# Three conversions moved behind attention's last copy, and two kinds of differences moved from VectorE to GpSimd

## The chip, the cores and the metric

One core of a Trainium2 chip runs one program that holds three stages: attention, a first mixture layer (MoE 1) and a second one (MoE 2). The metric is the time of the program on the device in microseconds; for the kernel before it is the median of three runs. TensorE, VectorE, ScalarE, GpSimd and SyncE are called PE, DVE, ACT, POOL and SP below, as in the profile's rows; SP issues all the DMAs that matter here.

## The reference

Attention has 4 x 8 heads of 576 rows and 64 columns: a causal softmax `a` over scores of q and k, then `local = a @ v`; beside it a memory term `phi(q) @ M_prev` divided by `phi(q) @ z_prev`, and a gate per head that mixes the two. The result, 2304 tokens x 512, is x for MoE 1: `g = x @ w_gate; h = silu(g) * (x @ w_val); x = h @ w_out` with 1536 hidden columns. MoE 2 has 8 experts with 1024 hidden columns, each `relu(x @ w1) @ w2`, weighted by a matrix that eight rounds of normalisation make from `exp(x @ w_gate)`.

The weights of MoE 1 arrive as 64-bit floats and are turned into 32-bit ones on the chip. Every product in full precision is made from three matmuls of "fp32r" halves: a value v is kept as a high half, which is v rounded to fp32r, and a low half, which is v minus the high half.

## The kernel before

**How the work is laid out.** Attention runs 16 pairs of heads through a hand-written software pipeline. The string ORDER lists the steps of a pair in the steady part, BEGIN and END are the lists for its two ends. In the last step of a pair (`values`, line 497 and on) the sums for the first 64 rows are copied from PSUM to x by DVE (`self.copy(9, ...)`, shown by the profile as `xacc<-pt`, 128x64), and the other 512 rows by ACT. Line 91 is the line of a helper through which all instructions of attention go: it pins instructions of the steady part to the order in which they are written.

**The conversion of MoE 1's weights.** There are 36 tiles of 128x512, sorted so that a hidden block f gets its gate tile, its value tile and, one block later, its out tile. Counted from one, tiles 1, 2 are gate and value of block 0, tiles 3, 4 those of block 1, tile 5 the out tile of block 0, tiles 6, 7 gate and value of block 2, tile 8 the out tile of block 1, and so on. A tile goes through these steps:

- a DMA of 512 KB on SP's queue into one of 4 buffers (`graw`, line 564);
- ACT makes a scaled magnitude (`na<-graw`, line 570), and POOL clamps it (`na<-na`, line 572, called the clamp below);
- five operations of DVE put the bits together (`narrow`, lines 550, 552, 554, 556 and 558); the first waits for the clamp, the fourth is the last reader of the `graw` buffer;
- ACT casts the high half, and DVE makes the low half (line 626 in `load_units`; in the rows `gw<-nb,gw` for gate and value tiles and `ws<-nb,ws` for out tiles, at line 91);
- SP stores the tile (gate and value tiles) and both halves to DRAM for later use (lines 625 and 627).

Tiles 1 to 3 are converted inside attention at hand-chosen places. From tile 4 on, `load_units` writes the steps down after attention's loop, where nothing pins them: the framework's planner gives each engine its order, by priorities and its own estimate of when an operand is ready, and an engine then works strictly in that order.

**MoE 1 while tiles are converted.** The first two chunks of 512 tokens are run together, one pass per block f (12 passes): `hidden` of chunk 0 (24 matmuls for gate and value, `p<-xs,gw`), then `second` of the block before (12 matmuls, `po<-h,ws`), then `hidden` of chunk 1 (24 matmuls). After each `hidden` ACT makes silu of the gate's sums and DVE multiplies by the value's sums, reading PSUM (line 758, `sg` and `hf`, called the gating product below). It frees two of the four PSUM banks that `hidden` uses in turn. For chunk 0 the result is split at once (`halves`, lines 777 and 778: ACT the high half of h, DVE the low half); the block's `second` uses it nearly a whole pass later. The part of the kernel behind these passes uses the same function `halves`, and is not touched.

Of the kernel before, what the change touches and what calls it, by code (L numbers as in the profile page):

```python
# [58 lines left out]
COPIES = "AAAAVVAVAVA"  # L59
# [17 lines left out]
class Ordered:  # L77
# [5 lines left out]
    def __getattr__(self, name):  # L83
        of = getattr(self.nc, name)
        if name in ("tensor", "scalar", "vector", "gpsimd"):
            return Ordered(of, self.tc, self.on)
        if not callable(of):
            return of

        def call(*args, **kw):  # L90
            ins = of(*args, **kw)  # L91
            return self.tc.keep_in_program_order(ins) if self.on() else ins

        return call

# [35 lines left out]
def f32(ap):  # L131
    return ap.bitcast(F32)
# [26 lines left out]
class Kernel:  # L159
# [285 lines left out]

    def copy(self, n, out, src):

        (self.nc.scalar.copy if COPIES[n] == "A" else self.nc.vector.tensor_copy)(out, src)

    def split(self, t, src):  # L450

# [143 lines left out]
    def load_units(self):  # L595


        nc = self.nc
# [3 lines left out]
        for n, (f, a) in enumerate(RAW):  # L602
# [11 lines left out]
            raw, w = begun[n]  # L614
            if n >= len(narrowed):
                b = self.nbp.tile([P, 512], F32, name="nb")
                for step, _ in enumerate(self.narrow(raw, w, b)):
                    if step == 1:
                        nc.scalar.copy(parts[:, 0], w)
                w = b  # L620
            else:
                nc.scalar.copy(parts[:, 0], w)
                w = narrowed[n]
            if a < 2:
                nc.sync.dma_start(self.keptw[f][:, a], w)
            nc.vector.tensor_sub(parts[:, 1], w, f32(parts[:, 0]))
            nc.sync.dma_start(kept, f32(parts))
            yield

# [99 lines left out]
    def moe1(self, last):  # L729
# [3 lines left out]
        with ExitStack() as st, ExitStack() as waiting, ExitStack() as banks:  # L733
# [38 lines left out]
                    half(ps[a], f, a, xs)  # L772
                return gated((savep if name == "hf" else sp).tile([P, 512], F32, name=name)[:, 0:n], *ps)

            def halves(hf, n):
                h = hp.tile([P, 2, 512], F32R, name="h")[:, :, self.columns(n)]
                nc.scalar.copy(h[:, 0], hf)
                nc.vector.tensor_sub(h[:, 1], hf, f32(h[:, 0]))  # L778
                return h[:, 0], h[:, 1]

            def second(po, f, h, shared=False):
# [32 lines left out]
            xs1 = self.split_x(*CHUNKS1[1], xsp1)  # L814
            for f in range(NF1):
                on()
                h = halves(hidden(f, xs, n, "sg"), n)
                on()
                if pend:
                    second(po, *pend)  # L820
                else:
                    po = new(n)
                pend = (f, h)
                on()
                saved.append(hidden(f, xs1, n, "hf"))
# [750 lines left out]
```

## Time and profile before

| what | us |
|---|---|
| median of three runs (2125.29 to 2129.17) | 2127.64 |
| the profiled execution's own time | 2126.93 |
| span of its records | 2125.2 |

Rows of the timeline hold: start in us from the span's start, duration in us, engine, source line, operation, the tile written <- the tiles read, shapes, the number of instructions merged into the row, and in square brackets how long the engine had been idle and what released it. Rows of windows hold: the stretch, its length, and for each engine its busy us with the count of instructions, then the granted TensorE clock (1.00 is full), the share of the DMA engines' time and GB/s. "SPq" is SP's queue of DMA issues.

### The profile page before, as it was taken

The numbers are of one execution on the slowest core, as the hardware profiler recorded it, in microseconds if no ns is written. First come the engines' busy times: TensorE is split into PE (matmuls) and PEld (weight loads), VectorE is DVE, ScalarE is ACT, GpSimd is POOL, SyncE is SP. The second block draws the span as 40 slices with busy tenths as digits, with TensorE's granted clock in tenths as the row PEclk, the third lists the DMA queues.
The fourth block names the chain that finished last, engine by engine and source line by source line (L and its number), as shares of the span: only waits on it lengthen the run. The fifth ranks groups of instructions, "written<-read, shape, count | busy, mean of one in ns | idle before, by whom it ended". The sixth has DMA issues, their size and how long they took to land.

```text
span 2125.2 us, 40534 instructions
## 1 busy us (share of the span) xinstructions
PE 2075.8 (98%) x15848; PEld 1914.1 (90%) x15848; DVE 1710.2 (80%) x3195; ACT 973.7 (46%) x1912; POOL 545.8 (26%) x464
## 2 busy tenths in 40 slices
PE   7999999999999999999999999999999999999999
PEld 5666677878879789999999999999999999999998
DVE  7898788675454667888988888888888888888887
ACT  7998533343332423434444444444444444444442
POOL 6888655000010042121221221212212122121210
PEclk9999899999999999999999999999999999999999
DMA  5342577466567836576475664756647566475564
GB/s 189 117 136 81 188 260 260 151 217 218 186 248 258 288 118 238 167 240 211 158 248 170 238 213 147 257 176 230 217 153 247 180 226 217 158 243 201 194 209 159
DMA packets 123358, 425.76 MB, mean 200 GB/s; under 512 B 13600, under 2 KB 13600, under 8 KB 120096
## 3 DMA queue, kind: packets, MB, share of 16 engines
q1 hardware_dynamic: 123168, 423.17, 58.6%
q8 instruction: 126, 2.06, 0.4%
q14 instruction: 64, 0.52, 0.1%
HBM read 374.36 MB, written 48.76 MB: 199 GB/s over the span
## 4 chain that ended last, share of the span: by engine, by line
PE 73%; DVE 16%; DMA 4%; ACT 3%; POOL 2%; issue 2%; SPq 0%; POOLq 0%; DVEq 0%; ACTq 0%
PE pu L1396 15%; PE pc L1233 14%; PE pq L1396 10%; PE pt L1233 10%; PE po L541 5%; PE pt L1319 4%; PE p L541 4%; PE pc L541 3%; DVE m L1249 2%; DVE xacc L1402 2%; PE pq L541 2%; PE pt L541 2%; DMA xr<-xp 2%; DVE h L1218 2%; PE po L91 2%
## 5 line engine op out<-in xcount | busy, mean ns | idle before, releaser
L1396 PE MATMUL pu<-xl,h 128*128 128x256 f32 x3240 | 424.4, 278 | 2.8 <-DVE xacc L1402 2.3
L1233 PE MATMUL pc<-xr,w 128*128 128x256 f32 x3072 | 395.7, 278 | 3.6 <-DMA xr<-xp 1.7
L1396 PEld LDWEIGHTS pu<-xl,h 128*128 128x128 f32 x3240 | 392.9, 188 | 7.0 <-DVE xacc L1402 4.1
L1233 PEld LDWEIGHTS pc<-xr,w 128*128 128x128 f32 x3072 | 372.3, 189 | 6.7 <-ACT m L1240 2.0
L1396 PE MATMUL pq<-xl,h 128*128 128x256 f32 x2430 | 317.0, 277 | 0.0
L1233 PE MATMUL pt<-xr,w 128*128 128x256 f32 x2304 | 295.6, 277 | 0.9 <-DMA xr<-xp 0.9
L1396 PEld LDWEIGHTS pq<-xl,h 128*128 128x128 f32 x2430 | 294.0, 188 | 0.3
L1217 ACT CAST h<-m 128x512 fp32r<-128x512 f32 (+1 forms) x345 | 190.4, 556 | 200.0 <-DVE m L1249 192.4
L1233 PEld LDWEIGHTS pt<-xr,w 128*128 128x128 f32 x2304 | 278.6, 188 | 2.0 <-DVE h L1215 1.1
L1402 DVE SCALAR_TENSOR_TENSOR xacc<-pu,Pw,xacc 128x256 f32<-128x256 f32 x540 | 236.8, 474 | 39.2 <-PE pu L1396 39.1
L1240 ACT COPY m<-pc 128x512 f32<-128x512 f32 x192 | 112.1, 584 | 255.0 <-PE pc L1233 253.3
L1402 DVE SCALAR_TENSOR_TENSOR xacc<-pq,Pw,xacc 128x256 f32<-128x256 f32 x405 | 177.4, 473 | 47.3 <-PE pq L1396 47.3
L1139 POOL TENSOR_TENSOR ws<-raw 128x512 f32<-128x512 f32 x62 | 83.8, 1364 | 499.3 <-DMA raw<-w 156.5
L1218 DVE TENSOR_TENSOR h<-m,h 128x512 fp32r<-128x512 f32 (+1 forms) x345 | 207.1, 624 | 1.6
L1249 DVE SCALAR_TENSOR_TENSOR m<-m 128x512 f32<-128x512 f32 x240 | 185.9, 775 | 16.6 <-ACT m L1276 13.1
L1214 ACT ACTIVATE h<-m 128x512 fp32r<-128x512 f32 x192 | 121.4, 632 | 169.9 <-DVE m L1245 168.7
L541 PE MATMUL p<-xs,gw 128*128 128x512 f32 (+1 forms) x864 | 172.8, 357 | 6.1 <-DVE sg L758 3.4
L1245 DVE TENSOR_TENSOR m<-pt,m 128x512 f32<-128x512 f32 x192 | 131.2, 683 | 54.8 <-ACT m L1240 52.9
L541 PEld LDWEIGHTS p<-xs,gw 128*128 128x128 f32 x864 | 143.6, 189 | 33.3 <-DVE sg L758 5.4
L1215 DVE SCALAR_TENSOR_TENSOR h<-m,h 128x512 fp32r<-128x512 f32 x192 | 146.9, 765 | 8.2 <-ACT h L1214 7.8
L1126 POOL TENSOR_TENSOR w<-raw,w 128x512 fp32r<-128x512 f32 x17 | 42.0, 2473 | 432.4 <-ACT w L1125 432.4
L541 PE MATMUL po<-h,ws 128*128 128x512 f32 x576 | 144.1, 391 | 2.0 <-DVE h L778 1.2
(224 smaller groups left out, 2966.7 us busy)
## 6 DMA issues: line engine op xcount, KB each, us to landing
xr<-xp SPq DMA_DIRECT2D x480, 512.0 KB, 4.1
raw<-w SPq DMA_DIRECT2D x64, 512.0 KB, 7.1
gw<-kg SPq DMA_DIRECT2D x24, 1024.0 KB, 7.0
graw<-gvo SPq DMA_DIRECT2D x36, 512.0 KB, 4.9
xp<-xl SPq DMA_DIRECT2D x30, 512.0 KB, 3.8
kg<-gw SPq DMA_DIRECT2D x24, 512.0 KB, 4.0
ws<-ko SPq DMA_DIRECT2D x24, 512.0 KB, 3.4
qk<-qkv SPq DMA_DIRECT2D x16, 640.0 KB, 4.9
```

Source lines behind the costliest of these rows:

```text
L541: self.nc.tensor.matmul(out, lhs[a], rhs[b], start=start and n == 0, stop=stop and n == 2, skip_group_check=shared)
L1214: nc.scalar.activation(hi, src, AF.Relu)
L1215: self.later(1, lambda: nc.vector.scalar_tensor_tensor(lo, src, 0.0, f32(hi), op0=ALU.max, op1=ALU.subtract))
L1217: nc.scalar.copy(hi, src)
L1218: self.later(1, lambda: nc.vector.tensor_sub(lo, src, f32(hi)))
L1233: self.marks[3] = nc.tensor.matmul(out[:, j * HT:(j + 1) * HT], w[:, a, j, k], x[:, b, k], start=start and j + k + n == 0, stop=k + n == 3 ...
L1240: self.marks[1] = nc.scalar.copy(t, src)
L1245: nc.vector.tensor_add(t, a, b)
L1249: relu = lambda out, a, b, op: nc.vector.scalar_tensor_tensor(out, a, 0.0, b, op0=ALU.max, op1=op)
L1319: nc.tensor.matmul(ph[:, j * HT:(j + 1) * HT], w[:, b, j, k], x[:, c, k], start=j + a + k + m == 0, stop=a + k + m == 4, skip_group_check= ...
L1396: nc.tensor.matmul(po[:, c], h[a][:, x, j, c * P:(c + 1) * P], w2[b][:, y, j], start=start and c + j + n == 0, stop=j + n == 3, skip_group ...
L1402: self.marks[2] = nc.vector.scalar_tensor_tensor(acc, po[:, c], self.Pw[:, at, e:e + 1], acc, op0=ALU.mult, op1=ALU.add)
```

## The change

Three edits:

- DVE's five operations of `narrow` for tiles 4, 5 and 6 get an order edge: none may be issued by DVE before the last DVE copy of attention's last pair (`last_move`, the last `self.copy` that DVE makes). The edge is one of order on DVE alone; ACT's cast, POOL's clamp and the DMAs of these tiles have none. The planner may still place everything else, tile 7's steps too.
- The low halves of out tiles (a = 2, 12 of them) are made by POOL. The low halves of gate and value tiles stay on DVE.
- The low halves of h in the 12 passes of MoE 1 during which tiles are converted are made by POOL; all other calls of `halves` stay on DVE.

The change of `Ordered.call` only makes it return the instruction in both cases.

```diff
         def call(*args, **kw):
             ins = of(*args, **kw)
-            return self.tc.keep_in_program_order(ins) if self.on() else ins
+            if self.on():
+                self.tc.keep_in_program_order(ins)
+            return ins
...
     def copy(self, n, out, src):
-        (self.nc.scalar.copy if COPIES[n] == "A" else self.nc.vector.tensor_copy)(out, src)
+        if COPIES[n] == "A":
+            self.nc.scalar.copy(out, src)
+        else:
+            self.last_move = self.nc.vector.tensor_copy(out, src)
...
             if n >= len(narrowed):
                 b = self.nbp.tile([P, 512], F32, name="nb")
-                for step, _ in enumerate(self.narrow(raw, w, b)):
-                    if step == 1:
-                        nc.scalar.copy(parts[:, 0], w)
+                with ExitStack() as order:
+                    if n < len(narrowed) + 3:
+                        order.enter_context(self.tc.issue_after(self.last_move.ins))
+                    for step, _ in enumerate(self.narrow(raw, w, b)):
+                        if step == 1:
+                            nc.scalar.copy(parts[:, 0], w)
                 w = b
...
-            nc.vector.tensor_sub(parts[:, 1], w, f32(parts[:, 0]))
+            (nc.vector if a < 2 else nc.gpsimd).tensor_sub(parts[:, 1], w, f32(parts[:, 0]))
...
-            def halves(hf, n):
+            def halves(hf, n, converting=False):
                 h = hp.tile([P, 2, 512], F32R, name="h")[:, :, self.columns(n)]
                 nc.scalar.copy(h[:, 0], hf)
-                nc.vector.tensor_sub(h[:, 1], hf, f32(h[:, 0]))
+                (nc.gpsimd if converting else nc.vector).tensor_sub(h[:, 1], hf, f32(h[:, 0]))
...
-                h = halves(hidden(f, xs, n, "sg"), n)
+                h = halves(hidden(f, xs, n, "sg"), n, True)
```

## Rows read from the trace of the kernel before

**Rows 1.** The page's first part: busy us, share of the span, instructions.
```profile
PE 2075.8 (98%) x15848; PEld 1914.1 (90%) x15848; DVE 1710.2 (80%) x3195; ACT 973.7 (46%) x1912; POOL 545.8 (26%) x464
```
**Rows 2.** Windows of 20 us: busy us of each engine, clock, DMA share, GB/s.
```profile
180.00:200.00 20.00, 19.42 (x159) 13.93 (x157) 18.99 (x42) 18.04 (x57) 17.13 (x21) 1.00 0.23 66
200.00:220.00 20.00, 17.86 (x109) 12.55 (x107) 12.83 (x28) 12.96 (x36) 12.05 (x18) 0.74 0.07 24
...
280.00:300.00 20.00, 16.84 (x68) 13.15 (x67) 15.64 (x30) 5.84 (x10) 11.48 (x4) 0.92 0.68 243
...
340.00:360.00 20.00, 20.00 (x89) 16.36 (x88) 17.16 (x31) 8.73 (x15) 9.00 (x4) 1.00 0.86 298
```
**Rows 3.** Timeline of PE, attention's last pairs and MoE 1's first matmuls.
```profile
188.79 2.37 PE L91 MATMUL po<-T,vm 128*64 128x128 f32 x16
...
201.47 2.37 PE L91 MATMUL po<-T,vm 128*64 128x128 f32 x16
...
206.52 0.47 PE L91 MATMUL ps<-KH,QH 64*128 64x448 f32 x2 [1.65 <-ACT P L91]
...
229.89 0.87 PE L91 MATMUL pt<-ident,P 128*128 128x128 f32 x3 [4.10 <-DVE xacc L91]
...
238.37 7.89 PE L541 MATMUL p<-xs,gw 128*128 128x512 f32 x34
```
**Rows 4.** Timeline of DVE in the same stretch.
```profile
204.44 0.43 DVE L550 TENSOR_SCALAR na<-na 128x512 int32<-128x512 int32 x1 [4.17 <-POOL na L91]
204.79 1.42 DVE L91 TENSOR_REDUCE nm<-ps 128x1 f32<-128x576 f32 x2
...
207.45 0.68 DVE L552 SCALAR_TENSOR_TENSOR na<-graw,na 128x512 int32<-128x512 int32 x1
...
227.59 0.83 DVE L550 TENSOR_SCALAR na<-na 128x512 int32<-128x512 int32 x1 [4.41 <-POOL na L572]
...
229.66 0.21 DVE L91 COPY xacc<-pt 128x64 f32<-128x64 f32 x1
...
234.80 1.17 DVE L550 TENSOR_SCALAR na<-na 128x512 int32<-128x512 int32 x2
...
237.81 0.23 DVE L91 COPY xacc<-pt 128x64 f32<-128x64 f32 x1 [1.24 <-PE pt L91]
```
**Rows 5.** Timeline of ACT: the exponentials behind DVE's first wait.
```profile
205.63 0.74 ACT L91 ACTIVATE P<-ps,nm 128x576 f32<-128x576 f32 x1 [3.39 <-DVE nm L91]
```
**Rows 6.** Windows of 2 us where the granted clock falls and rises.
```profile
208.00:210.00 2.00, 2.00 (x14) 1.67 (x14) 1.90 (x5) 0.67 (x2) 0.00 (x0) 0.56 0.00 0
...
218.00:220.00 2.00, 2.00 (x16) 1.45 (x16) 1.68 (x4) 1.72 (x5) 1.84 (x4) 0.88 0.31 109
...
228.00:230.00 2.00, 0.11 (x1) 0.14 (x2) 1.97 (x5) 0.00 (x0) 1.44 (x1) 0.68 0.00 0
...
234.00:236.00 2.00, 2.00 (x13) 1.27 (x14) 2.00 (x5) 0.15 (x1) 2.00 (x2) 0.62 1.02 287
```
**Rows 7.** Waits from 238 to 402 us: who waits, total us, times, longest.
```profile
PE p L541 <- DVE sg L758: 3.4, 4, 2.0
PE p L541 <- DVE hf L758: 2.6, 2, 1.5
...
DVE na L550 <- POOL na L572: 15.0, 9, 2.5
...
SPq L627 <- DVE ws L91: 25.4, 12, 3.9
```
**Rows 8.** Timeline of DVE: a difference beside one of POOL, and one alone.
```profile
238.99 1.68 DVE L533 TENSOR_TENSOR xs<-xacc,xs 128x512 fp32r<-128x512 f32 x1
...
344.20 0.68 DVE L778 TENSOR_TENSOR h<-sg,h 128x512 fp32r<-128x512 f32 x1
```
**Rows 9.** Timeline of POOL: two differences, and two clamps.
```profile
238.52 3.31 POOL L533 TENSOR_TENSOR xs<-xacc,xs 128x512 fp32r<-128x512 f32 x2 [1.86 <-ACT xs L531]
...
289.11 7.68 POOL L572 TENSOR_SCALAR na<-na 128x512 f32<-128x512 f32 x2 [2.58 <-ACT na L570]
```

## The prediction

> **What bounds the kernel now.** I read the page's first part, then windows, then the timelines of the two stretches that the change touches, then the waits. The page says that PE is busy 98% of the span [rows 1], so a change of some microseconds must come from the few places where PE is not busy or runs at the lower clock. The windows of 20 us show where these are near the change. In the middle of attention PE is busy 19.42 of 20 us with the clock at 1.00; from 200 to 220 it is 17.86 at 0.74 [rows 2]. In MoE 1 the stretch from 280 to 300 has 16.84 at 0.92, and from 340 to 360 PE is full again [rows 2].
>
> The two holes in attention's end have one shape. At 204.44 DVE starts the first `narrow` operation of tile 4 after 4.17 us in which it did nothing but wait for POOL's clamp [rows 4]. Behind it in DVE's order stands the maximum of the scores (204.79), behind that ACT's exponential, which had ACT idle for 3.39 us [rows 5], and PE lost 1.65 us before 206.52 [rows 3]. At 227.59 the same operation of tile 5 starts after 4.41 us of waiting for its clamp; behind it stands the small copy of 229.66, and PE waited 4.10 us for exactly that copy [rows 3, 4]. Neither tile is needed by PE before MoE 1, so both waits are pure loss. After each hole the granted clock falls to 0.50, the 1.2 GHz level: in the windows from 208 to 220 it is 0.56, four times 0.50, and 0.88, which makes 2 x (0.44 + 4 x 0.50 + 0.12) = 5.1 us of full-speed time not granted; from 228 to 236 it is 0.68, twice 0.50, and 0.62, which makes 3.4 us [rows 6].
>
> In MoE 1 PE waits for the gating products only: 3.4 + 2.6 = 6.0 us [rows 7], and the 0.92 of one window costs another 20 x 0.08 = 1.6 us [rows 2], some 8 us in all. There too the products are late because they stand behind the first operation of `narrow`, which waited nine times, 15.0 us together, for clamps [rows 7].
>
> **The change part by part.** *The order edge.* It removes from attention's end what stands at both holes. Twelve operations are affected: five each of tiles 4 and 5, and of tile 6 the first (one of the two in the row of 234.80) and the second. Gone with certainty, if nothing else blocks there, are the two idle times of PE: 1.65 + 4.10 = 5.75 us, the low end. If the clock also stays up and PE alone sets the pace, the 5.1 + 3.4 = 8.5 us come on top: 14.3 us, the high end. I can check that end: a steady pair takes 201.47 - 188.79 = 12.7 us [rows 3], and this stretch holds less PE work per pair than that. But the end of the pipeline is not PE alone: the last pairs pass from PE to ACT to DVE to POOL and back, with no other pair to fill in. Half of the clock's loss is what I take, 4.25 us, for 10.0 us together. So MoE 1's first matmul should start near 238.4 - 10.0 = 228.4 us.
>
> What is late next at those places: at the first, PE's transposes run until 204.9, so the maximum has the time to finish; at the second, ACT's copies of T. The clamps stay where POOL has them, and nobody in attention waits for them any more.
>
> *What the edge moves into MoE 1.* The twelve operations cost 8 x 0.68 + 4 x 0.43 = 7.2 us of DVE (0.68 and 0.43 from the rows of lines 552 and 550; the short line 554 is taken as 550) [rows 4]. They now stand behind the last copy, in the stretch where DVE is already 17.2 of 20 us busy [rows 2]. The `graw` buffers of tiles 4 to 6 come free that much later too, and so the loads of tiles 8 to 10. I cost PE's wait for weights at nothing: tile 4 is needed 60 matmuls after the start, that is 60 x 7.89 / 34 = 13.9 us [rows 3], and three tiles' `narrow` with its low halves is under 10 us. Without that cover PE would wait once for at most the difference in start, a few us. The gating products are where 7.2 us can show: at the ratio of the stage (6.0 us of PE's waits for 15.0 us of DVE's [rows 7], 0.4) it is 2.9 us.
>
> *The 24 low halves on POOL.* DVE loses 24 x 0.68 = 16.3 us of busy time [rows 8]. POOL gains 24 operations; the nearest rows are its own two differences of the same shape, 3.31 us for two, so 1.65 each and 40 us together [rows 9]. And they are not free for DVE: the DVE difference that ran beside these two took 1.68 instead of 0.68 us [rows 8]. So each moved one gives DVE 0.68 and takes between 0 (DVE idle, or at a gating product, of which one operand is in PSUM) and 1.0 us. I take 0.6, and DVE's balance is 24 x (0.6 - 0.68) = -1.9 us, nothing; the bounds are -16.3 and +7.7. POOL's queue is the other side: each clamp now has about two thirds of a difference (24 for 33 clamps) beside it, 1.2 us, and the next `narrow` stands behind the clamp. If the nine waits of DVE grow by half of that each, they make 9 x 0.6 = 5.4 us. POOL can be held off, too: two clamps took 7.68 us while DVE ran without a pause [rows 9]. Behind a late out tile SP's queue is held, which already waits 25.4 us for twelve of them with the next loads behind [rows 7]; a difference that ends 1 us later costs 12 us of SP's time, of which I put nothing on PE, since the wait for buffers that come free follows it anyway. DVE's sum is then 7.2 - 1.9 + 5.4 = 10.7 us, and at 0.4 it costs PE 4.3 us. Where the tiles are well ahead (340 to 360, PE full) it costs nothing, so I take 3 us for the stage; bounds are -8 (all waits of today gone) and +14 (below). The low half of h itself is not late: it has a pass less some 2 us until its `second`.
>
> The plumbing of `Ordered.call` and `copy` issues the same instructions and costs nothing.
>
> The rows show a difference of DVE stretched from 0.68 to 1.68 us beside those of POOL [rows 8, 9]. The Trainium skill, page "SBUF — State Buffer", section "SBUF: two separate sides", says that DVE operations with two SBUF inputs and GpSimd share a port pair that one holds for the whole instruction while the other fully blocks; the row agrees in kind, and by the rule each moved difference would hold DVE off for up to its whole 1.65 us, which is the price in the first rival.
>
> **The sum.** -10.0 + 3.0 = -7.0 us. The profiled execution took 2126.9 us (span 2125.2 and 1.7 around it), 0.7 under the median; the same 7.0 us taken from the median give 2120.6 us.
>
> **The rivals.** *The slower side: DVE and POOL block each other for the whole conversion.* If DVE, which does hardly anything else there than operations with two SBUF inputs, stands still for each moved difference, it loses 24 x (1.65 - 0.68) = 23 us instead of 1.9 gained, and the clamps come 1.2 us later at each of nine waits, 11 us; with the 7.2 moved this is 41 us, at 0.4 16.6 us for PE. Against the 10.0 us of the tail it is +6.6: 2134 us. It decides from a stage loss of 14.3 us on. For it speaks the 1.68 us row, against it that DVE waited 15.0 us for clamps and can lie idle while POOL works. The Trainium skill's page "Perfetto Trace Analysis", section "Optimizing Scalar/DVE Operations", warns that offloading between these two engines might not help.
>
> *The hole stays: tile 7 takes the place.* Tile 7 has no edge, and its first operation is the second one of the row of 234.80, already ahead of the last copy [rows 4]. With tiles 4 to 6 out of the way the planner can set it where tile 5's stood, waiting for a later clamp. Then the second hole with its clock (4.1 + 1.7 us) stays, the gain is 4.2 - 3.0 = 1.2 us: 2126.4 us. Against it: its clamp came after tile 6's, and the planner knows that order.
>
> *Both parts pay.* The tail gives 10.0, and with DVE relieved the products are in time, 8 us: 2109.6 us. For it speaks that the same kind of wait causes both; against it the 1.68.
>
> **How the numbers follow.** The forecast has 0.52, the slower rival 0.17, the hole that stays 0.18, both parts paying 0.13. What this kernel's measurement can tell from no change is about 0.2%, 4.3 us, so faster means under 2123.4 and slower over 2131.9. Of the forecast 0.04 lies above 2123.4 (a tail gain near 5.75); of the slower rival 0.03 stays under 2131.9. Faster: 0.48 + 0.13 = 0.61; within: 0.04 + 0.18 + 0.03 = 0.25; slower 0.14. The forecast's own range is 2113 to 2125 (tail 14.3 or 5.75, with 3 in the stage). The range to hold 8 in 10 reaches from the case in which both pay, 2109, to the middle of the slower rival, 2133.
>
> **What would show it.** Right: no wait of line 550 for a clamp on DVE before the last `xacc<-pt` copy; PE's row with 4.10 gone; `p<-xs,gw` starting between 224 and 233 us, with the clock near 1.00 in the windows before. In the stage: POOL's differences at 1.3 to 1.7 us, DVE's neighbours over 1 us, PE's waits for `sg` and `hf` near 9 us instead of 6.0. Wrong: a DVE wait for any other clamp ahead of attention's copies; MoE 1's matmuls starting on time but its twelve passes longer by 14 us or more; or a clock that falls at attention's end although the holes are gone, which would leave the tail at 5.75.

## The result and the profile after

The changed kernel takes 2141.03 us (median of four runs, 2138.32 to 2141.88), the kernel before beside it 2128.40: a ratio of 1.0067 as estimated from the runs, interval [1.0051, 1.0083] (the two medians alone give 1.0059). The change makes the kernel slower; 2120.6 was forecast. The profiled execution took 2138.32 us with a span of 2136.5, 11.3 more than before. The page's first part of the changed kernel (busy us, share of the span, instructions) shows hardly anything of it:

```profile
PE 2073.8 (97%) x15848; PEld 1908.9 (89%) x15848; DVE 1718.5 (80%) x3171; ACT 972.7 (46%) x1912; POOL 570.1 (27%) x488
```

Against [rows 1], DVE has 24 instructions less and is busy 8.3 us longer, where 16 us less would be the plain arithmetic. The windows of 20 us (columns as in [rows 2]) show where the time went:

```profile
200.00:220.00 20.00, 18.95 (x141) 12.79 (x140) 15.81 (x30) 18.20 (x48) 17.02 (x23) 1.00 0.18 67
...
280.00:300.00 20.00, 17.16 (x69) 13.73 (x68) 14.65 (x25) 6.30 (x11) 11.15 (x7) 0.91 0.73 239
300.00:320.00 20.00, 15.15 (x60) 12.09 (x59) 16.89 (x24) 6.17 (x11) 13.13 (x8) 0.91 0.71 235
340.00:360.00 20.00, 14.03 (x60) 10.63 (x59) 15.61 (x25) 6.20 (x11) 14.07 (x7) 1.00 0.71 240
```

From 200 to 220 PE does more than before and keeps the full clock: attention's end has gained. From 300 to 320, where PE had 19.13 us before, and from 340 to 360, where it was full [rows 2], it now has 15.15 and 14.03 of 20 us. The timeline of PE (columns as in the front's rows) gives the two ends of the stage and what PE waits for in it:

```profile
228.44 0.73 PE L91 MATMUL po<-Z,vmr 128*128 128x512 f32 x2 [2.92 <-DVE Z L91]
229.01 16.49 PE L546 MATMUL p<-xs,gw 128*128 128x512 f32 x72
...
285.25 9.94 PE L546 MATMUL p<-xs,gw 128*128 128x512 f32 x36 [2.84 <-DVE hf L766]
...
305.49 10.04 PE L546 MATMUL p<-xs,gw 128*128 128x512 f32 x36 [4.85 <-DVE hf L766]
...
420.86 3.34 PE L546 MATMUL po<-h,ws 128*128 128x512 f32 x14
```

MoE 1 starts at 229.01 instead of 238.37 [rows 3], 9.4 us earlier. The last `second` of the twelve passes starts at 420.86; in the kernel before it is the 409.04 of the rows further down. So the passes (first matmul to last `second`) take 191.8 us instead of 170.7, 21.2 more. -9.4 + 21.2 = +11.8; behind the passes both kernels take the same 1716 us, to 0.5. The whole result is these two terms. In the passes PE's idle time grows from 6.1 to 22.1 us, and the granted clock takes some 5 us against 2 before (0.91 in the windows of 280, 300 and 360, against 0.92 and 0.99 in those of 280 and 300): together some 19 of the 21.2.

The waits of the changed kernel from 229 to 413 us (who waits for whom, total us, times, longest):

```profile
POOL ws L91 <- DVE nb L563: 27.2, 9, 5.0
POOL na L577 <- ACT na L575: 26.1, 12, 4.1
...
DVE na L555 <- POOL na L577: 20.3, 16, 3.4
...
PE p L546 <- DVE hf L766: 14.0, 6, 4.9
...
PE p L546 <- DVE sg L766: 4.5, 4, 2.7
...
PE po L546 <- POOL h L786: 1.6, 3, 0.7
```

(Lines have moved: 550 is now 555, 552 is 557, 554 is 559, 556 is 561, 558 is 563, 572 is 577, 758 is 766.) PE's waits for the gating products have grown from 6.0 us [rows 7] to 18.5, DVE's for clamps from 15.0 to 20.3, and POOL has a new one of 27.2 us, for DVE. The last line is small but new too: three times a `second` of PE waits for the low half of h. How they hang together is seen in the timelines of POOL and DVE:

```profile
280.24 1.29 POOL L91 TENSOR_TENSOR ws<-nb,ws 128x512 fp32r<-128x512 f32 x1 [3.72 <-DVE nb L563]
281.50 1.92 POOL L577 TENSOR_SCALAR na<-na 128x512 f32<-128x512 f32 x1
...
299.33 1.60 POOL L91 TENSOR_TENSOR ws<-nb,ws 128x512 fp32r<-128x512 f32 x1 [3.09 <-DVE nb L563]
300.90 4.23 POOL L577 TENSOR_SCALAR na<-na 128x512 f32<-128x512 f32 x2
```

```profile
225.59 0.43 DVE L555 TENSOR_SCALAR na<-na 128x512 int32<-128x512 int32 x1 [4.28 <-POOL na L577]
...
283.44 0.43 DVE L555 TENSOR_SCALAR na<-na 128x512 int32<-128x512 int32 x1 [3.36 <-POOL na L577]
...
284.51 0.68 DVE L766 TENSOR_TENSOR hf<-hf,p 128x512 f32<-128x512 f32 x1
...
299.82 1.66 DVE L563 TENSOR_TENSOR nb<-na,nb 128x512 f32<-128x512 f32 x1
...
303.28 0.82 DVE L555 TENSOR_SCALAR na<-na 128x512 int32<-128x512 int32 x1 [1.81 <-POOL na L577]
...
304.75 0.68 DVE L766 TENSOR_TENSOR hf<-hf,p 128x512 f32<-128x512 f32 x1
...
386.55 0.69 DVE L563 TENSOR_TENSOR nb<-na,nb 128x512 f32<-128x512 f32 x1
```

Follow 280 to 285. POOL stands 3.72 us at an out tile's difference, which waits for DVE's last `narrow` operation; it takes 1.29 us; only then comes the next tile's clamp. DVE waits 3.36 us for that clamp, the gating product stands behind it (284.51), and PE goes on at 285.25 after 2.84 us. At 299.33 the other effect joins: beside POOL's difference DVE's operation of line 563 takes 1.66 instead of 0.69 us, two clamps follow, and PE waits 4.85 us at 305.49. The 386.55 is the last tile's last operation of `narrow`. The 225.59 is tile 7's first one, ahead of attention's last copy: one of the forecast's rivals, which cost PE the 2.92 us of the row of 228.44.

### The profile page after: what moved, and what is told of

Its sections match the earlier page's. It is cut to its first block, busy times and chain, and to the rows that moved or that the text cites. A ratio compares the mean times of both kernels' runs of the same rounds, so it can differ in the third digit from the quotient of the medians.

```text
span 2136.5 us, 40525 instructions
## 1 busy us (share of the span) xinstructions
PE 2073.8 (97%) x15848; PEld 1908.9 (89%) x15848; DVE 1718.5 (80%) x3171; ACT 972.7 (46%) x1912; POOL 570.1 (27%) x488
## 4 chain that ended last, share of the span: by engine, by line
PE 68%; DVE 12%; DMA 4%; POOL 2%; issue 2%; ACT 1%; SPq 0%; POOLq 0%; ACTq 0%; DVEq 0%
PE pu L1404 15%; PE pc L1241 14%; PE pq L1404 11%; PE pt L1241 10%; PE po L546 4%; PE pt L1327 4%; PE p L546 3%; PE pc L546 2%; PE pq L546 2%; DVE xacc L1410 2%; DVE m L1257 2%; PE pt L546 2%; DMA xr<-xp 2%; DVE h L1226 1%; DVE h L1223 1%
## 5 line engine op out<-in xcount | busy, mean ns | idle before, releaser
L1147 POOL TENSOR_TENSOR ws<-raw 128x512 f32<-128x512 f32 x62 | 83.8, 1362 | 499.6 <-DMA raw<-w 171.4
L1257 DVE SCALAR_TENSOR_TENSOR m<-m 128x512 f32<-128x512 f32 x240 | 186.0, 775 | 15.2 <-ACT m L1284 11.8
L546 PE MATMUL p<-xs,gw 128*128 128x512 f32 (+1 forms) x864 | 177.6, 362 | 20.5 <-DVE hf L766 14.0
```

The costliest lines, as they stand in the source:

```text
L546: self.nc.tensor.matmul(out, lhs[a], rhs[b], start=start and n == 0, stop=stop and n == 2, skip_group_check=shared)
L1257: relu = lambda out, a, b, op: nc.vector.scalar_tensor_tensor(out, a, 0.0, b, op0=ALU.max, op1=op)
```

## The experiments

All kernels below are timed against the kernel before on the same chip. Lines may be shifted by up to 5 in kernels with added code. The diffs of e1 to e4, e5 and e11 are against the changed kernel, those of the others against e1 (e8 against e4, e15 and e16 against e5 and e11). "Path" is the time from MoE 1's first matmul to the start of the last tile's last `narrow` operation (line 563), "passes" that to the last `second`, both from one profiled execution each; the ratio and its interval are estimated from all timed runs.

| kernel | path us | passes us | ratio, interval |
|---|---|---|---|
| before | 136.0 | 170.7 | 1 |
| changed | 157.5 | 191.8 | 1.0067 [1.0051, 1.0083] |
| e1 edge only | 141.1 | 175.8 | 0.9993 [0.9982, 1.0005] |
| e2 both differences on POOL, no edge | 148.3 | 182.6 | 1.0052 [1.0032, 1.0072] |
| e3 edge, h on POOL | 144.4 | 178.8 | 1.0001 [0.9988, 1.0014] |
| e4 edge, out tiles on POOL | 151.2 | 185.5 | 1.0031 [1.0019, 1.0043] |
| e5 edge on tile 7 too | 136.3 | 170.9 | 0.9955 [0.9940, 0.9970] |
| e6 edge, POOL waits | 142.3 | 176.9 | 0.9999 [0.9987, 1.0011] |
| e7 edge, POOL reads | 151.5 | 186.1 | 1.0032 [1.0018, 1.0047] |
| e8 as e4, differences later | 150.7 | 185.4 | 1.0042 [1.0027, 1.0056] |
| e9 edge, store waits for POOL | 143.1 | 179.1 | 1.0001 [0.9992, 1.0010] |
| e10 edge, POOL fills | 145.3 | 179.9 | 0.9994 [0.9983, 1.0004] |
| e11 changed, tile 7 too | 157.5 | 191.8 | 1.0053 [1.0038, 1.0068] |
| e12 edge, out tiles' lows by ACT | 140.3 | 175.6 | 0.9998 [0.9988, 1.0007] |
| e13 edge, out tiles' lows short | 141.3 | 176.4 | 0.9994 [0.9985, 1.0003] |
| e14 edge, POOL waits and fills | 148.3 | 182.6 | 1.0018 [1.0006, 1.0029] |
| e15 as e5, clamps on DVE | 139.1 | 163.3 | 0.9918 [0.9905, 0.9931] |
| e16 as e11, clamps on DVE | 138.5 | 171.4 | 0.9951 [0.9937, 0.9966] |

Single executions of one kernel differ by several us, so the ratios carry the verdicts; path and passes say where. For instance MoE 1 starts between 228.6 and 232.1 us in the eleven other kernels that have the changed kernel's edge, and path and passes count from there: e9 and e10 have longer passes than e1, but they start 2.4 and 3.3 us before it and end only 1.0 and 0.8 us behind it. Differences between two experiments are taken between their medians below; the kernel before took 2125.8 to 2126.7 us beside them, 2128.4 beside the changed kernel.

### The parts of the change

**e1: the edge alone.** Both kinds of differences go back to DVE; this is the base of most later kernels.

```diff
-            (nc.vector if a < 2 else nc.gpsimd).tensor_sub(parts[:, 1], w, f32(parts[:, 0]))
+            nc.vector.tensor_sub(parts[:, 1], w, f32(parts[:, 0]))
-                h = halves(hidden(f, xs, n, "sg"), n, True)
+                h = halves(hidden(f, xs, n, "sg"), n)
```

> The order edge alone; all low halves on DVE as before. Figures of before and after: MoE 1's first matmul at 238.4 and 229.0 us, and from it to the last po<-h,ws of block 11 (the twelve passes) 170.6 and 191.9 us. Theory Q (queue): the passes got longer because the low halves stand in POOL's order ahead of clamps and wait there for DVE (27.2 us) and ACT, so that DVE gets the clamps late. Theory P (port): because POOL's differences hold off DVE's operations with two SBUF inputs (line 552/557 went from a mean of 678 to 820 ns). Theory M (moved work): because the twelve narrow operations and the late loads put the conversion behind. Q and P: first matmul near 229, passes 168 to 176 us, time 2116 to 2123 us. M: passes 185 us or more, time 2133 us or more. All: tile 7's first operation still waits for its clamp ahead of attention's last copy.

**e2: the differences alone**, and **e3, e4: the edge with one kind of difference each.**

```diff
-                    if n < len(narrowed) + 3:
+                    if n < 0:
```

> No order edge; both kinds of low halves on POOL. Q and P: first matmul near 238, passes 185 to 192 us, time 2142 to 2150 us, the slowest of all. M: passes 168 to 174 us, time near 2127.

```diff
-            (nc.vector if a < 2 else nc.gpsimd).tensor_sub(parts[:, 1], w, f32(parts[:, 0]))
+            nc.vector.tensor_sub(parts[:, 1], w, f32(parts[:, 0]))
```

> The order edge, and only the low halves of h on POOL; those of the out tiles on DVE. Q: h waits in POOL's queue for ACT alone (17.7 us in the changed kernel, against 31.2 for the out tiles), and its input is made before the next clamps are due: passes 172 to 178 us. P: it is half of the port's load, so half of the loss: passes 178 to 184 us.

```diff
-                h = halves(hidden(f, xs, n, "sg"), n, True)
+                h = halves(hidden(f, xs, n, "sg"), n)
```

> The order edge, and only the low halves of the out tiles on POOL; those of h on DVE. Q: these are the ones that wait for DVE ahead of a clamp, so most of the loss: passes 184 to 192 us, DVE waiting for clamps 18 us or more. P: half of the loss, as with h alone: passes 178 to 184 us.

Measured: e1 2125.49 us, e2 2138.29, e3 2127.27, e4 2133.34 beside 2126.42. The edge alone gains nothing that can be told from no change: what attention's end gives, the path in MoE 1 gives back (+5.1 us against before) and tile 7's hole keeps (DVE waits 4.27 us for its clamp here too). The differences alone lose 11.9 us. With the edge, those of h add 1.8 us to e1, those of the out tiles 7.8, both together 15.5 (13.6 if each kernel is taken against the kernel before beside it). So the loss lies in the 24 differences, most of it in the 12 of the out tiles. The two kinds together seem to cost more than their sum of 9.6, but hardly beyond the intervals. Of the theories, M falls: e1's passes are far from its 185 us, and e2's are long without an edge. Q and P had both put e2 at 185 us or more (182.6 came) and e1 under 2123 us; e3's passes are in P's range and e4's in Q's.

**What the table shows of the stage.** In 13 of the 16 experiments, before and after, the last `second` starts 34.3 to 35.4 us behind the last tile's last `narrow` operation, whatever the passes took. These are the timelines' rows of the kernel before (DVE's, then PE's) and, third, that of e1 (DVE's; its last `second` starts at 407.7):

```profile
374.41 0.69 DVE L558 TENSOR_TENSOR nb<-na,nb 128x512 f32<-128x512 f32 x1
```
```profile
409.04 3.34 PE L541 MATMUL po<-h,ws 128*128 128x512 f32 x14
```
```profile
373.07 0.69 DVE L563 TENSOR_TENSOR nb<-na,nb 128x512 f32<-128x512 f32 x1
```

409.04 - 374.41 = 34.6; after the change 420.86 - 386.55 = 34.3; in e1 34.6. (The exceptions are e9 with 36.1, e15 with 24.3 and e16 with 32.9.) The distance alone does not say which of the two engines leads; the waits do. Up to that operation DVE waits in none of the 18 traces for PE, only for clamps and other steps of POOL and ACT (in the kernel before 15.0 us, all for clamps [rows 7]), while PE waits for DVE's products. So in these 15 kernels the twelve passes end a fixed time after DVE has converted the last tile, and what lengthens DVE's path lengthens the passes one for one.

**e5: tile 7 behind the copy too**, with all differences on DVE, and **e11: the same edge on the changed kernel.**

```diff
-                    if n < len(narrowed) + 3:
+                    if n < len(narrowed) + 4:
```

> As e1 (order edge, all low halves on DVE), with the edge also on tile 7. In e1 tile 7's first operation stood ahead of attention's last copy and DVE waited 4.27 us for its clamp there. Expected by every theory: that wait and PE's 2.9 us behind it are gone, MoE 1's first matmul near 226 us. Theory M (the edge lengthens the passes, 175.8 us in e1 against 170.6 before, because the narrow operations and the loads behind them come later): passes 176 to 180 us, time as e1 or 1 us less. If the passes stay at 172 to 176, time 2121 to 2123.

> The changed kernel with tile 7's edge added: e5 with both kinds of low halves on POOL. The tail gains what e5 gained over e1 (first matmul near 226 us), the passes keep the loss of the 24 differences, 12 to 16 us over e5's 170.9. Passes 183 to 190 us, time 2130 to 2137 us. If the loss came from the edge and the differences together only through tile 7's hole, passes would be 175 or less and the time under 2123.

e5 takes 2117.20 us beside 2126.67 and beats both kernels: the first matmul of MoE 1 starts at 225.9, 12.5 us earlier than before, and the path is no longer than before. e11 takes 2137.04 beside 2125.81: its first matmul comes at 225.4, but path and passes are those of the changed kernel. So the hole at tile 7 is worth some 3 us at attention's end, and the loss in the passes doesn't depend on it. Why e5's path is 4.8 us shorter than e1's, and the time better than the 2121 that was expected at best, is not settled: DVE's order of operations is another one there, and DVE waits 7.0 us for clamps instead of 15.5.

### What in a moved difference costs

Four properties of a moved difference could do it: it makes POOL wait for DVE ahead of the next clamps (Q), it takes POOL's time (T), its store waits for POOL (S), or its reads hold DVE off at SBUF, which means that DVE's operations take longer beside it (P). Each was given to e1 by itself.

**e6: the wait alone**: a difference of 8 columns per out tile, which writes to a place of its own.

```diff
+            if a == 2:
+                dum = self.dump.tile([P, 8], F32, name="dum")
+                nc.gpsimd.tensor_sub(dum, w[:, 0:8], f32(parts[:, 0])[:, 0:8])
...
```

> e1, plus on POOL a difference of 8 columns per out tile that reads what the low half would read and writes to nowhere: POOL waits for DVE's fifth operation at that place, but does no work to speak of. DVE still makes all low halves. Q: the wait ahead of the clamps is the cost: passes 182 to 188 us (e4 had 185.5), POOL waiting for DVE's nb 20 us or more. P: no port load, so passes as e1, 174 to 178 us. What the out tile's store does on SP's queue is as in e1.

**e7: the reads alone**: 12 products of POOL of the full shape on data that nobody touches, each behind the out tile's clamp; DVE keeps its own differences.

```diff
...
+            if a == 2:
+                still = self.x[:, 3, 1536:2048].rearrange("p (j n) -> p j n", j=4)
+                with self.tc.issue_after(self.clamps[n].ins):
+                    nc.gpsimd.tensor_mul(still, still, self.ones.unsqueeze(1).to_broadcast([P, 4, P]))
```

> e1, plus on POOL per out tile a product of 128x512 of two tiles that lie still (x times one, over x), ordered behind that tile's clamp: the port load of e4 without its wait for DVE. DVE still makes all low halves. Q: passes 175 to 179 us. P: 12 times up to 1.0 us for DVE without the 8.2 us that e4 takes off it: passes 182 to 188 us, and lines 555 to 563 longer by 50 to 100 ns in the mean.

**e8: another order**: e4 with each out tile's difference behind the clamps of the next two tiles.

```diff
...
+            if a < 2:
+                nc.vector.tensor_sub(parts[:, 1], w, f32(parts[:, 0]))
+            else:
+                with self.tc.issue_after(self.clamps[min(n + 2, len(RAW) - 1)].ins):
+                    nc.gpsimd.tensor_sub(parts[:, 1], w, f32(parts[:, 0]))
```

> e4 (order edge, low halves of out tiles on POOL), but each of these low halves is ordered on POOL behind the clamps of the next two tiles, where in the changed kernel it often stood right ahead of the next tile's clamp. Q: the loss goes: passes 174 to 179 us, DVE waiting for clamps 14 us or less. P: the load on the port is the same: passes 183 to 188 us.

**e9: the store alone**: 8 of 512 columns of an out tile's low half on POOL, so that the store waits for POOL.

```diff
+            if a == 2:
+                nc.vector.tensor_sub(parts[:, 1, 8:512], w[:, 8:512], f32(parts[:, 0, 8:512]))
+                nc.gpsimd.tensor_sub(parts[:, 1, 0:8], w[:, 0:8], f32(parts[:, 0, 0:8]))
+            else:
+                nc.vector.tensor_sub(parts[:, 1], w, f32(parts[:, 0]))
```

> What stands after eight runs: POOL waiting for DVE ahead of clamps costs nothing by itself (e6, passes 176.9 us against 175.8 in e1), so Q falls; POOL's load alone costs 10 us (e7), but there DVE kept its work. Still to be told apart for the out tiles' low halves (e4: passes 185.5): theory P (the port), theory T (POOL's time: the clamp behind starts 1.3 us later, whatever the port), theory S (the store of an out tile waits for POOL on SP's queue, 43.0 us in e4 against 21.8 in e1, and the loads of the next tiles stand behind it). This run is e1 with 8 of the 512 columns of each out tile's low half on POOL and 504 on DVE: the wait of POOL and the wait of the store without load on the port. S: passes 181 to 187 us. P and T: 174 to 178 us.

**e10: POOL's time alone**: two fills per out tile, which read nothing, behind its clamp.

```diff
...
+            if a == 2:
+                with self.tc.issue_after(self.clamps[n].ins):
+                    for _ in range(2):
+                        nc.gpsimd.memset(f32(parts[:, 1]), 0.0)
```

> e1, plus two fills of 128x512 with zeros on POOL per out tile, ordered behind that tile's clamp, over the place where DVE then writes the low half: POOL's time without a read of SBUF. T: the next clamp is as late as with e7's product, so passes 180 to 186 us if the fills take 0.6 us or more each. P and S: 174 to 178 us, and DVE's mean durations as in e1.

e6 takes 2125.76, e9 2127.57 and e10 2124.93 us: waiting alone, the store and POOL's time alone cost nothing that can be told from no change. In e6 the wait is really there: POOL waits 27.9 us for DVE, as it does in the changed kernel (27.2). e8 (2136.63) does not gain on e4, so a later place of the difference in POOL's order doesn't help. e7 takes 2134.53: reads alone, without any wait, cost 9.0 us against e1. DVE's order of operations in e6, e7 and e10 is that of e1, instruction by instruction, so the planner's order is no cause there. The groups by line of DVE (busy us, mean ns, idle before and what ended it) of e7:

```profile
L561 DVE SCALAR_TENSOR_TENSOR nb<-graw,nb 128x512 f32<-128x512 uint32 x33 | 25.7, 787 | 0.3
...
L555 DVE TENSOR_SCALAR na<-na 128x512 int32<-128x512 int32 x31 | 22.4, 722 | 12.8 <-POOL na L577 12.8
```

They stand against 692 and 551 ns in e1 (the latter is in a fence below). DVE waits no longer for clamps (12.8 us, 15.5 in e1); its operations themselves are longer.

**e14: wait and time together, no large read**: e6's difference of 8 columns, and two fills of 128x512 behind it.

```diff
+            if a == 2:
+                dum = self.dump.tile([P, 8], F32, name="dum")
+                nc.gpsimd.tensor_sub(dum, w[:, 0:8], f32(parts[:, 0])[:, 0:8])
+                for _ in range(2):
+                    nc.gpsimd.memset(begun[n][1], 0.0)
...
```

> The kernel with the edge alone, in which POOL does for each out tile a difference of 8 columns that waits for the tile's last narrow operation and behind it two fills of 128x512 that read nothing (1.2 us): the wait and the time of a moved difference together, without its reads. Waiting alone and time alone cost nothing measurable. Theory QT (the two together make the clamps late): DVE waits for clamps 20 us instead of 16, 2132. Theory P (the reads of two operands in SBUF are what costs): 2125 to 2127.

2129.79 us, 4.3 over e1: between the two theories. The groups of POOL, and behind them a wait of ACT from the same stretch:

```profile
L577 POOL TENSOR_SCALAR na<-na 128x512 f32<-128x512 f32 x29 | 71.2, 2467 | 24.0 <-ACT na L575 21.4 <-DVE gw L91 2.6
L91 POOL MEMSET na<- 128x512 f32 x24 | 13.2, 551 | 0.6
L91 POOL TENSOR_TENSOR dum<-nb,ws 128x8 f32<-128x8 f32 x12 | 8.6, 714 | 31.5 <-DVE nb L563 26.5 <-ACT h L790 5.0
```
```profile
ACT na L575 <- POOL na L91: 13.8, 3, 6.0
```

The 8 columns take 714 ns on average (0.20 at the least, 1.72 at the most), so with its fills POOL is held 714 + 2 x 551 = 1.8 us per out tile behind a wait for DVE, somewhat more than the 1.48 us of a real difference. DVE's waits for clamps rise from 15.5 to 17.9 us. But the fills go into the out tile's `na` buffer, and the ACT step that writes this buffer next waits for them three times, 13.8 us together, which it does not do in e1 or after a real difference. So e14 does not isolate wait and time: together they cost at most some 4 of the 7.8 us of e4, and how much of that is the buffer is not shown.

### Whether DVE's time decides

**e12 and e13** take the out tiles' low halves off DVE; in e12 ACT makes a copy of the high half in their place, in e13 DVE makes 8 columns.

```diff
+            if a == 2:
+                nc.scalar.copy(parts[:, 1], f32(parts[:, 0]))
+            else:
+                nc.vector.tensor_sub(parts[:, 1], w, f32(parts[:, 0]))
```

> e1 without the out tiles' low halves as such: in their place ACT copies the high half, so the values are wrong and DVE loses 8.2 us of work with nothing on POOL. If DVE's time sets the passes (P), they get shorter by 3 to 8 us: 168 to 173 us, time 2118 to 2123. If the clamps or loads set them (T, S), they stay at 174 to 178.

```diff
...
+            if a == 2:
+                with self.tc.issue_after(self.clamps[n].ins):
+                    nc.gpsimd.memset(f32(parts[:, 1]), 0.0)
+                nc.vector.tensor_sub(parts[:, 1, 0:8], w[:, 0:8], f32(parts[:, 0, 0:8]))
+            else:
+                nc.vector.tensor_sub(parts[:, 1], w, f32(parts[:, 0]))
```

> The kernel with the edge alone, with the low half of an out tile made by DVE for 8 of 512 columns only (the rest is left zero by one fill of POOL behind the tile's clamp, so the output is not the reference's). Takes some 12 x 0.6 = 7 us off DVE without loading ACT. In every kernel so far the twelve passes last as long as DVE's way from attention's last copy to the last tile's last narrow operation, plus 34 us. If DVE's own time decides that way (theory D), it is 7 us shorter: 135 us instead of 142, time 2118.5. If the clamps and loads decide it (rival L), DVE only waits longer for clamps, 22 us instead of 16, and the time stays at 2125.

2124.86 and 2125.11 us: neither gains on e1, and the paths are the same within 1 us. In e12 DVE waits 18.0 us for clamps instead of 15.5. So time that is taken off DVE went into waiting in e12, which goes against theory D. It is no proof: ACT has a copy more there and the planner's order is another one. And e13 does not test it, because it relieves nothing: the short operations still take 0.216 us, 12 x (0.68 - 0.22) = 5.6 us off, but beside the fills the others are longer, and DVE's path without its idle time is as long as in e1, to 0.5 us.

Why freed time should turn into waiting is seen in the waits themselves. In the kernel before (DVE's timeline; POOL's row of these clamps is in [rows 9]):

```profile
292.45 0.68 DVE L556 SCALAR_TENSOR_TENSOR nb<-graw,nb 128x512 f32<-128x512 uint32 x1
294.94 0.82 DVE L550 TENSOR_SCALAR na<-na 128x512 int32<-128x512 int32 x1 [1.81 <-POOL na L572]
```

The clamp began at 289.11, 4.0 us before DVE stopped, and ended 1.81 us after it; a clamp by itself takes 1.91. So next to nothing of it was done while DVE ran. Six of DVE's nine waits in the kernel before are of this kind, 1.81 us each behind a clamp that had begun 0.4 to 4.0 us ahead of the pause. There DVE does not wait because POOL is late; POOL gets to its clamp when DVE stops for it.

**e15 and e16: the 29 clamps on DVE**, with the edge up to tile 7: e15 with all differences on DVE, e16 with the 24 on POOL.

```diff
-        nc.gpsimd.tensor_scalar(t, t, pattern(0x40000000), pattern(0x4FEFFE00), op0=ALU.max, op1=ALU.min)
+        (nc.vector if dve else nc.gpsimd).tensor_scalar(t, t, pattern(0x40000000), pattern(0x4FEFFE00), op0=ALU.max, op1=ALU.min)
...
-                for _ in self.clamp(*begun[-1]):
+                for _ in self.clamp(*begun[-1], n + 2 > 6):
```

> The kernel with the edge on tiles 4 to 7, low halves on DVE, and the 29 clamps of tiles 8 to 36 on DVE too, so that POOL does nothing in the conversion. DVE gets 29 operations like line 555, 0.43 us each, 12.5 us, and loses its waits for POOL's clamps (7 us) and the hold-off beside them (8 us summed over the operations that ran beside a clamp): -3 us, 2114. Rival: the hold-off is small or DVE then waits for ACT in the clamps' place: +5 us, 2122.

> The changed kernel (24 differences on POOL) with the edge on tile 7 too and the 29 clamps of tiles 8 to 36 on DVE: POOL makes the differences and nothing else. Against the same kernel with clamps on DVE and differences on DVE. Theory H (hold-off cancels what DVE is relieved of, and the loss comes from clamps that are late): differences cost within 3 us, 2114 to 2118. Theory P (the hold-off is itself the loss): still 10 us or more over it, 2125.

e15 takes 2108.81 us beside 2126.20, the fastest of all, 8.4 under e5; e16 takes 2115.88. The groups of DVE in e15:

```profile
L563 DVE TENSOR_TENSOR nb<-na,nb 128x512 f32<-128x512 f32 x33 | 22.5, 683 | 0.0
...
L555 DVE TENSOR_SCALAR na<-na 128x512 int32<-128x512 int32 x33 | 13.7, 418 | 0.0
L577 DVE TENSOR_SCALAR na<-na 128x512 f32<-128x512 f32 x29 | 12.2, 422 | 7.4 <-ACT na L575 7.2
```

Nothing is held off any more, and a clamp takes DVE 0.42 us where POOL took 2.0 to 2.7 on average. With its 12.2 us the path is 2.8 us longer than e5's, but it no longer decides: the passes take 163.3 us, PE's waits are 1.5 us. In e16 the path is as short as in e15 (138.5): with no clamp behind POOL's differences, what they take from DVE and what they free cancel. Still e16 is 7.1 us slower, and the waits of PE in it (7.6 us, 1.5 in e15) say by what:

```profile
PE p L546 <- DVE hf L766: 4.2, 4, 1.8
PE po L546 <- POOL h L786: 2.7, 2, 1.4
PE p L546 <- DVE sg L766: 0.7, 1, 0.7
```

In the kernels with clamps on POOL the same 24 differences cost 2137.04 - 2117.20 = 19.8 us (e11, e5). Theory H had forecast 3 for e16 and theory P 10 or more; 7.1 lies between them.

## Why the prediction was wrong, point by point

**The edge: right in size, not in its parts.** -10.0 was forecast for MoE 1's start, -9.4 came. The clock indeed stays up (1.00 from 200 to 220, where it was 0.74), so my half of the clock's loss was too careful; and the second rival, tile 7 in the hole's place, came as well and took 2.92 us back. e5, without that hole, has 12.5. That -9.4 came so near -10.0 is luck: one error gave roughly what the other took, and single executions with the same edge differ by 3.5 us in this start.

**"The 24 low halves on POOL": the step that failed.** For the stage +3.0 was forecast, +21.2 came, outside my bound of +14; MoE 1 starting on time with passes longer by 14 us or more was one of my signs of being wrong. Two parts of the step are to be told apart.

*The ratio of 0.4.* I had read it from the kernel before as PE's 6.0 us of waits per 15.0 of DVE's, and applied it to what the change adds. But that is an average over a stage in which the passes end a fixed time behind DVE's path. At the margin the ratio is 1: path +21.5, passes +21.2. e1 shows it without any moved difference: path and passes both grow by 5.1, where I had charged PE 2.9 of 7.2. (By my own rows the twelve operations are seven long and five short ones, 6.9 us. What they cost is not fixed either: e5 moves more of them, and its path is as long as before, because DVE's waits for clamps fall by 8 us.) The page's 98% for PE had led me away from it: PE was busy, and yet not what the stage's end hung on.

*The sum of DVE.* I had 10.7 us: 7.2 moved, 5.4 more of waiting for clamps, and -1.9 as the balance of the differences. The path's 21.5 split into 5.1 of e1 and 16.4 of the differences, for which my terms were 5.4 - 1.9 = 3.5. Adding up the gaps in the rows of DVE's timeline from attention's last copy to the last `narrow` operation gives 16.5 us of idle time in e1 and 24.9 after the change; the rest of that stretch is 125.8 and 133.8 us. So about half of this loss is waiting (+8.4) and half work (+8.0), although DVE has lost the differences.

The work half is the hold-off. DVE's groups of the changed kernel and of e1:

```profile
L557 DVE SCALAR_TENSOR_TENSOR na<-graw,na 128x512 int32<-128x512 int32 x32 | 26.2, 820 | 0.4
...
L555 DVE TENSOR_SCALAR na<-na 128x512 int32<-128x512 int32 x31 | 21.7, 701 | 20.3 <-POOL na L577 20.3
L91 DVE TENSOR_TENSOR gw<-nb,gw 128x512 fp32r<-128x512 f32 x21 | 17.5, 855 | 0.1
L559 DVE TENSOR_SCALAR nb<-na 128x512 int32<-128x512 int32 x33 | 16.6, 505 | 2.9 <-POOL ws L91 2.6
```
```profile
L557 DVE SCALAR_TENSOR_TENSOR na<-graw,na 128x512 int32<-128x512 int32 x32 | 23.1, 728 | 0.0
...
L555 DVE TENSOR_SCALAR na<-na 128x512 int32<-128x512 int32 x31 | 17.1, 551 | 15.5 <-POOL na L577 15.5
L559 DVE TENSOR_SCALAR nb<-na 128x512 int32<-128x512 int32 x33 | 15.0, 461 | 0.2
L91 DVE TENSOR_TENSOR gw<-nb,gw 128x512 fp32r<-128x512 f32 x21 | 14.3, 699 | 0.0
```

These four groups and lines 561 and 563 (24.2 and 26.5 us after, 22.6 and 22.4 in e1) are the same 183 instructions in both kernels: 132.7 us against 114.5, +18.2, where the 24 differences had taken 16.4 (8.2 for each kind in e1). That is 0.76 us per moved difference against the 0.6 that I took and the 0.68 that it frees: a small error, but the relief is gone entirely. Up to the last `narrow` operation, where 20 of the 24 differences stood in e1 (13.6 us), the operations that stayed are 17.0 us longer, so the durations give +3.3; the other 4.7 of the +8.0 is overlap, for operations in an unbroken row overlap by 0.08 us in the records (252.00 and 252.60 below are 0.68 us long), and after the change fewer do. One place shows the hold-off in both directions, first POOL, then DVE:

```profile
251.29 2.55 POOL L91 TENSOR_TENSOR ws<-nb,ws 128x512 fp32r<-128x512 f32 x1 [1.60 <-DVE nb L563]
254.01 1.53 POOL L786 TENSOR_TENSOR h<-sg,h 128x512 fp32r<-128x512 f32 x1 [0.17 <-ACT h L785]
```
```profile
252.00 0.68 DVE L563 TENSOR_TENSOR nb<-na,nb 128x512 f32<-128x512 f32 x1
252.60 0.68 DVE L766 TENSOR_TENSOR sg<-sg,p 128x512 f32<-128x512 f32 x1
253.20 1.18 DVE L91 TENSOR_TENSOR gw<-nb,gw 128x512 fp32r<-128x512 f32 x1
254.30 1.78 DVE L557 SCALAR_TENSOR_TENSOR na<-graw,na 128x512 int32<-128x512 int32 x1
```

POOL's difference takes 2.55 us while DVE runs without a pause, where the shortest take 1.28; the gating product, which reads PSUM, is not touched; the next operation of DVE takes 1.18 us, and the one beside the difference of h 1.78 instead of 0.68. The Trainium skill, page "SBUF — State Buffer", section "SBUF: two separate sides", describes such a pair of ports as a lock that one of the two engines holds for a whole instruction, for VectorE's operations with two SBUF inputs and for those in a 2-port mode; these rows agree for the first kind. Operations of line 555, which read one tile, go from 0.42 to 1.51 us too; in which mode they run no row shows. The Trainium skill's page "Perfetto Trace Analysis", section "Optimizing Scalar/DVE Operations", says that offloading between these two engines might not help; in e2 it costs 11.9 us.

The waiting half is the clamp in POOL's queue: it stands behind a difference that waits for DVE, as at 280.24. My 5.4 us for it was near the +5.3 of the waits' rows (20.3 for 15.0), by luck: I had let nine waits grow by 0.6 us each, and there are 16 that are shorter on average. "Two clamps took 7.68 us while DVE ran without a pause" was misread as well: DVE paused for 1.81 us in it, for just this clamp. What I had not priced are the 2.6 us in which line 559 waits for POOL to be done with an out tile's `nb` buffer, and the handovers beside them. And the low half of h, which I had called not late, cost PE 1.6 us.

**The rivals.** The first, "DVE and POOL block each other for the whole conversion", is nearest to what came: 2134 was its price, 2141 the time. Its size was again too small by the ratio: of its 41 us of DVE, half came, and PE paid that in full instead of 0.4 of it. "Both parts pay" is out: DVE was not relieved. The range of my forecast also had a slip: 14.3 us from the tail with 3 in the stage gives 2116, not 2113, which does not bear on the miss.

**What stays open.** How much of the out tiles' 7.8 us belongs to the hold-off and how much to the clamp's delay: e7 (reads without wait, DVE not relieved) costs 9.0, e14 (wait and time without reads, but with waits for a buffer) 4.3, and the two are not additive parts of one thing. A rival stands beside both: the planner also gave DVE's other operations another order in each kernel with moved differences (e2 to e4, e8, e11, e16 and the changed one) than in the kernel it is compared with, and no run with moved differences holds that order fixed. Only e6, e7 and e10 have e1's order, so the hold-off by reads is shown by itself, and the rest of the loss is not cleared of the order. Why h alone costs only 1.8 us is shown in part: in e3 DVE's waits for clamps do not grow (13.0 us, 15.5 in e1), in e4 they do (19.5), since no `nb` buffer and no `narrow` hangs on h's difference; its hold-off is there all the same (line 561 takes 794 ns, 692 in e1).

## What to carry to other kernels

Look for what a stage's end keeps a fixed distance to, across two or three variants, and see in the waits which side leads: here it was the last converted tile, 34 us ahead of the last `second` in nearly all of them, and every microsecond on that path counted in full though the page has PE 98% busy. Don't price what a change adds by the average share of waits that reaches the bounding engine; that share is of the slack already used up. When DVE waits for a short operation of POOL, try that operation on DVE (here 12 us more of work, 8.4 us faster) rather than more of DVE's work on POOL.

## What was not expected of the hardware

- A clamp on POOL beside a busy DVE takes 2.0 to 2.7 us on average in these kernels, 1.91 at the least and 7.8 at the most; the same clamp on DVE takes 0.42 us. Taking it away also brings DVE's own operations of line 555 from 0.55 us (e1) to 0.418 (e15), so POOL's operations with one tile to read hold DVE off too.
- A difference of 8 columns takes POOL 0.20 to 1.72 us in e14, 0.71 on average: beside a busy DVE even a tiny operation of POOL can be held off longer than the 1.28 us that 512 columns take at the least.
- Fills of POOL, which read nothing, hold off DVE's operations with one tile to read rather than those with two: in e10 line 559 takes 0.538 us on average, line 555 0.584 and line 561 0.699, against 0.461, 0.551 and 0.692 in e1. The kernel's time does not show it.
